# Attention and highway FFN on one core: the first duo by query blocks, the FFN in pairs of blocks, the last block in two column halves

## The chip, the cores and the metric

The kernel runs on one NeuronCore of a Trainium2 chip. The metric is the device time of one execution in microseconds (us). The time before the change is 175.32 us, the median of three runs (174.87 to 175.51). A profiled execution gives the trace that is read below; its span, from the first to the last instruction, is 173.5 us, and the granted TensorE clock is 0.987 on the mean.

Engines: PE is TensorE (PEld its weight loads), DVE VectorE, ACT ScalarE, POOL GpSimd, SP SyncE. Lxxx is a line of the kernel.

## The reference

Eight batches with eight heads of 576 positions and 64 dimensions go through sliding-window attention with an ALiBi bias. The heads are then joined to rows of 512, and each row goes through a highway layer with two 512 x 512 weights.

```python
def _attn_ref(q, k, v):                       # (8, 8, 576, 64) float32 each
    scale = 1.0 / np.sqrt(D); window = 128
    scores = scale * np.matmul(q, k.transpose(0, 1, 3, 2))
    rel = pos[:, None] - pos[None, :]
    slopes = 2.0 ** (-8.0 * (np.arange(H) + 1) / H)
    scores = np.where((rel >= 0) & (rel < window), scores - slopes * abs(rel), -1e9)
    attn = softmax(scores)
    return np.matmul(attn, v)

def _moe_ref(x, w_h, w_t, b_t):               # x: (4608, 512)
    H = np.maximum(x @ w_h, 0.0)
    T = 1.0 / (1.0 + np.exp(-(x @ w_t + b_t)))
    return T * H + (1.0 - T) * x              # = x + T * (H - x)
```

## The kernel before

Two batches make a duo (r = 0, 1), and there are four duos (m = 0 to 3). The 576 positions are four query blocks of 128 and a tail of 64; because of the window, block qb needs the keys of blocks qb - 1 and qb alone. A duo is worked through in stages, each of which names its pieces as (key block, query block, column):

```python
    STAGES = {
        "A": ((0, 0, 0), (0, 1, 128), (1, 1, 256), (1, 2, 384)),
        "B": ((2, 2, 0), (2, 3, 128), (3, 3, 256), (3, 4, 384), (4, 4, 448)),
        "a": ((0, 0, 0), (0, 1, 128)),
        "b": ((1, 1, 0), (1, 2, 128)),
        "c": ((2, 2, 0), (2, 3, 128)),
        "d": ((3, 3, 0), (3, 4, 128), (4, 4, 192)),
    }
    ORDER = ("abcd", "AB", "AB", "AB")
    GROUPS = {
        "A": ((0,), (1,), (2,), (3,)), "B": ((0,), (1,), (2,), (3,), (4,)),
        "a": ((0,), (1,)), "b": ((0,), (1,)), "c": ((0,), (1,)), "d": ((0,), (1,), (2,)),
    }
```

Loads of q, k and v go through GpSimd's DMA queue, which casts them from float32 to bfloat16. A q or k load takes four neighbouring positions to one partition, so a row of it is 256 elements; a V load takes 64. The first duo's first half comes in quarters by groups of heads. The weight w_h comes by SyncE in float32 ahead of everything and is cast by ScalarE.

```python
    def load_qk(m, w, x=None, hs=None):
        ...   # "h (p t) d -> p h (t d)", t=4: rows of 256 elements
            nc.gpsimd.dma_start(out=o, in_=i)
    def load_wf():
        nc.sync.dma_start(out=w_stage()..., in_=moe_w_h...)
    def cast_wf():
        nc.scalar.copy(out=wH[:]..., in_=w_stage())
```

For a stage and two heads (g): TensorE transposes q and k, makes the scores in two halves of 64 rows (one for each batch of the duo), ScalarE takes exp, VectorE multiplies with the mask, TensorE multiplies with V, which has a column of ones, and VectorE divides.

```python
                nc.tensor.transpose(out=pt[...], in_=L[ps, r, nh * hs + hl, ...], identity=ident[ps, ps])   # L271
                nc.tensor.matmul(out=sc[:, r, ...], lhsT=KT[...], rhs=rhs, ...)        # L329
        nc.scalar.activation(out=PT[...], in_=SC[...], func=ACTF.Exp, ...)             # L345
        nc.vector.tensor_tensor(out=o, in0=o, in1=mk..., op=ALU.mult)                  # L364
                            nc.tensor.matmul(out=av[...], lhsT=pt[...], rhs=va[...])   # L393
        nc.vector.reciprocal(...)                                                      # L409
        nc.vector.tensor_tensor(out=x..., in0=av..., in1=rd..., op=ALU.mult)           # L410
```

The FFN works on one block of 128 rows at a time (36 of them):

```python
                nc.tensor.transpose(out=pt[:, c * P : (c + 1) * P], ...)     # f_x, 4 of them, L433
        nc.scalar.copy(out=xt..., in_=TR...)                                 # f_xe, L442
            nc.tensor.matmul(out=AH, lhsT=XT..., rhs=wH[:, c, :], ...)       # f_h, 4, L449
        nc.vector.scalar_tensor_tensor(out=uu, in0=AH..., scalar=0.0, in1=x,
            op0=ALU.max, op1=ALU.subtract)                                   # f_u, L456
            nc.tensor.matmul(out=az, lhsT=XT..., rhs=wT[:, c, :], ...)       # f_z, 4, L465
        nc.tensor.matmul(out=az, lhsT=ones1[:], rhs=bT[:], ...)              # the bias, L467
        nc.scalar.activation(out=tt, in_=AZ..., func=ACTF.Tanh, scale=0.5)   # f_th, L473
        eng.tensor_scalar(out=tt, in0=tt, scalar1=0.5, scalar2=0.5, ...)     # f_t, L478
        nc.vector.tensor_tensor(out=uu, in0=uu, in1=tt, op=ALU.mult)         # f_g, L483
        eng.tensor_tensor(out=ot, in0=uu, in1=x, op=ALU.add)                 # f_out, L489
            nc.sync.dma_start(out=dst[t], ...)                               # f_st, 4, L505 (tail: 2, L497)
```

PSUM is one tile of eight banks, handed out bank by bank. The order of all steps and the bank of each are fixed lists of numbers in the kernel (ISSUE, BANKS), found beforehand; each engine keeps that order, and semaphores do the rest.

Of the kernel before, what the change touches and what calls it, by code (L numbers as in the profile page):

```python
# [14 lines left out]
def kernel(  # L15
# [30 lines left out]
        "a": ((0, 0, 0), (0, 1, 128)),  # L46
        "b": ((1, 1, 0), (1, 2, 128)),
        "c": ((2, 2, 0), (2, 3, 128)),
        "d": ((3, 3, 0), (3, 4, 128), (4, 4, 192)),
    }  # L50
    ORDER = ("abcd", "AB", "AB", "AB")
    DMA_X = ()

    HOME = {"A": ("A", 0), "B": ("B", 0), "a": ("A", 0), "b": ("A", 256), "c": ("B", 0), "d": ("B", 256)}

    GROUPS = {
        "A": ((0,), (1,), (2,), (3,)), "B": ((0,), (1,), (2,), (3,), (4,)),
        "a": ((0,), (1,)), "b": ((0,), (1,)), "c": ((0,), (1,)), "d": ((0,), (1,), (2,)),
    }

    ADD_MASK = ()
# [36 lines left out]
    def load_qk(m, w, x=None, hs=None):  # L98
        src, dst = ((q, QL), (k, KL))[w]
        ps = slice(0, P) if x is None else slice(64 * x, 64 * x + 64)  # L100
        for r in (slice(0, 2),) if hs is None else (0, 1):
            hh = slice(0, H) if hs is None else slice(4 * hs, 4 * hs + 4)
            if hs is None:
                o = dst[m % 2][ps].rearrange("p r h n -> p (r h) n")
                i = src[2 * m : 2 * m + 2, :, 4 * ps.start : 4 * ps.stop, :].rearrange(
                    "r h (p t) d -> p (r h) (t d)", t=4
                )
            else:
                o = dst[m % 2][ps, r, hh, :]
                i = src[2 * m + r, hh, 4 * ps.start : 4 * ps.stop, :].rearrange(  # L110
                    "h (p t) d -> p h (t d)", t=4
                )
            nc.gpsimd.dma_start(out=o, in_=i)  # L113
# [22 lines left out]
    MKA = ADD_MASK and cp.tile([P, H, 2 * P], BF16, name="mka")  # L136
    cvec = cp.tile([P, H], F32, name="cvec")
    ones1 = cp.tile([P, P], BF16, name="ones1")
    wH = cp.tile([P, NCK, DM], BF16, name="wH")
# [25 lines left out]


    BIG = float(2**20)

    def c_mka():
        nc.vector.tensor_scalar(out=MKA[:, :, 0:P], in0=bc(tri[:, 0, :], P), scalar1=BIG,  # L170
                                scalar2=-BIG, op0=ALU.mult, op1=ALU.add)
        for h in range(H):
            nc.vector.tensor_scalar(
# [127 lines left out]
    def width(kind):  # L301
        return 512 if kind in "AB" else 256
# [489 lines left out]
```

The softmax here doesn't subtract the row's maximum and nothing guards it: scores larger than these inputs give would overflow.

## Time and profile before

| what | before |
|---|---|
| time, median of 3 (lowest to highest) | 175.32 us (174.87 to 175.51) |
| profiled span | 173.5 us |
| TensorE busy | 150.3 us, 87% |
| VectorE busy | 140.0 us, 81% |
| ScalarE busy | 125.4 us, 72% |
| GpSimd busy | 118.1 us, 68% |
| DMA, GpSimd's queue | 62,832 packets, 14.68 MB |
| DMA, stores and w_h | 7,312 packets, 10.49 MB |

Busy time is the time in which an engine has an instruction in work. For TensorE it says little of how well it is filled, since matmuls overlap in its pipeline: the distance from one start to the next tells more. The groups of the profile give an instruction's line, engine, operation, tiles and count, then busy time and mean time of one, then the idle time ahead of it and what ended that. The chain is followed back from the last instruction, at each step to what released it.

### The profile page before, as it was taken

What the parts mean: (1) busy time and instruction counts of PE and PEld (TensorE: products, weight loads), DVE (VectorE), ACT (ScalarE), POOL (GpSimd) and SP (SyncE); (2) the same over time, 40 slices, a digit from 0 to 9 for tenths busy, and PEclk for the clock granted to TensorE, in tenths of its full rate; (3) what the DMA queues carried; (4) which work ended last, traced back from release to release, by engine and by line L of the source; (5) the groups of instructions that cost most, each with busy time, mean ns of one, the idle gap of its engine ahead of it and who ended that gap; (6) DMA issues with size and microseconds to landing.
All of it is one profiled execution on the core that took longest, in us unless ns stands there. A gap on an engine that the chain in (4) does not pass through costs nothing.

```text
span 173.5 us, 5255 instructions
## 1 busy us (share of the span) xinstructions
PE 150.3 (87%) x2132; PEld 92.8 (54%) x2132; DVE 140.0 (81%) x244; ACT 125.4 (72%) x178; POOL 118.1 (68%) x132
## 2 busy tenths in 40 slices
PE   0169789999799789999999979999999999999930
PEld 0158544666566347766556755566556556754410
DVE  5087686999898888999867999889887899976580
ACT  2625678797799969899779968799898897235510
POOL 7997373488883799984067985884485969676540
PEclk9999999999999999999999999999999999999995
DMA  4999999999999999999999996793124332454443
GB/s 161 211 191 191 154 197 185 184 176 102 190 205 202 197 108 158 216 217 210 252 118 154 153 179 97 88 135 99 45 64 121 76 90 68 107 127 113 125 121 91
DMA packets 70167, 25.50 MB, mean 147 GB/s; under 512 B 48128, under 2 KB 65024, under 8 KB 70144
## 3 DMA queue, kind: packets, MB, share of 16 engines
q0 software_dynamic: 62832, 14.68, 120.7%
q1 hardware_dynamic: 7312, 10.49, 22.6%
q8 instruction: 16, 0.26, 0.7%
q14 instruction: 7, 0.06, 0.1%
HBM read 30.41 MB, written 9.44 MB: 230 GB/s over the span
## 4 chain that ended last, share of the span: by engine, by line
PE 53%; DMA 29%; DVE 5%; POOL 4%; ACT 3%; issue 2%; SPq 0%; POOLq 0%; ACTq 0%; DVEq 0%
DMA va<-in_v_dram 17%; PE ps L465 14%; PE ps L449 14%; DMA ktl<-in_k_dram 8%; PE ps L393 7%; PE ps L329 7%; PE ps L271 4%; PE ps L433 4%; DMA kl<-in_k_dram 3%; PE ps L467 3%; ACT pt L345 2%; DVE pt L364 1%; POOL kl L113 1%; DVE uu L456 1%; DMA out_dram<-ot 1%
## 5 line engine op out<-in xcount | busy, mean ns | idle before, releaser
L345 ACT ACTIVATE pt<-ps,bias 128x1024 bf16<-128x1024 f32 (+1 forms) x80 | 72.2, 950 | 13.5 <-PE ps L329 13.2
L489 POOL TENSOR_TENSOR ot<-uu,x 128x512 f32<-128x512 bf16 x35 | 47.7, 1365 | 24.9 <-DVE uu L483 24.8
L364 DVE TENSOR_TENSOR pt<-pt,mk 128x2048 bf16<-128x2048 bf16 (+1 forms) x40 | 46.5, 1174 | 0.8 <-ACT pt L345 0.8
L465 PE MATMUL ps<-wT,xt 128*128 128x512 bf16 x144 | 37.0, 379 | 1.0 <-DVE uu L456 0.8
L449 PE MATMUL ps<-wH,xt 128*128 128x512 bf16 x144 | 37.0, 386 | 0.3 <-DVE qt L290 0.3
L473 ACT ACTIVATE tt<-ps 128x512 f16<-128x512 f32 x36 | 21.6, 602 | 13.0 <-PE ps L467 11.9
L456 DVE SCALAR_TENSOR_TENSOR uu<-ps,x 128x512 bf16<-128x512 f32 x36 | 24.5, 684 | 4.6 <-PE ps L449 4.3
L329 PE MATMUL ps<-qt,kt 64*128 64x256 bf16 (+2 forms) x384 | 24.8, 248 | 3.4 <-DVE qt L290 1.1
L478 POOL TENSOR_SCALAR tt<-tt 128x512 f16<-128x512 f16 x32 | 21.8, 687 | 7.7 <-ACT tt L473 7.5
L410 DVE TENSOR_TENSOR x<-ps,rd 128x256 bf16<-128x256 f32 (+3 forms) x40 | 25.5, 638 | 1.4
L125 POOL DMA_DIRECT2D va<-in_v_dram x20 | 22.3, 1115 | 5.6 <-DMA ql<-in_q_dram 4.2
L393 PE MATMUL ps<-va,pt 128*128 128x65 bf16 (+1 forms) x576 | 24.9, 197 | 0.8 <-DMA va<-in_v_dram 0.7
L393 PEld LDWEIGHTS <-pt 128*128 128x128 bf16 (+1 forms) x576 | 21.1, 101 | 8.2 <-issue 2.9
L442 ACT COPY xt<-ps 128x512 bf16<-128x512 bf16 x36 | 20.7, 589 | 5.3 <-PE ps L433 5.1
L483 DVE TENSOR_TENSOR uu<-uu,tt 128x512 bf16<-128x512 bf16 x36 | 19.1, 538 | 4.3 <-POOL tt L478 4.1
L449 PEld LDWEIGHTS <-xt 128*128 128x128 bf16 x144 | 13.0, 99 | 14.3 <-issue 2.1
L465 PEld LDWEIGHTS <-xt 128*128 128x128 bf16 x144 | 12.9, 98 | 13.6 <-issue 1.5
L329 PEld LDWEIGHTS <-kt 64*128 64x128 bf16 x384 | 13.2, 96 | 12.9 <-issue 8.9
L271 PE MATMUL ps<-ident,kl 128*64 128x128 bf16 (+1 forms) x320 | 12.3, 228 | 8.1 <-DMA kl<-in_k_dram 7.9
L296 ACT COPY kt<-ps 128x1024 bf16<-128x1024 bf16 x13 | 13.0, 1020 | 5.4 <-PE ps L271 5.4
L271 PEld LDWEIGHTS <-kl 128*64 128x64 bf16 (+1 forms) x320 | 9.9, 126 | 10.1 <-DMA kl<-in_k_dram 8.4
L290 DVE COPY qt<-ps 128x1024 bf16<-128x1024 bf16 x16 | 11.0, 686 | 3.8 <-PE ps L271 3.7
(44 smaller groups left out, 125.5 us busy)
## 6 DMA issues: line engine op xcount, KB each, us to landing
out_dram<-ot SPq DMA_DIRECT2D x128, 64.0 KB, 2.4
va<-in_v_dram POOLq DMA_DIRECT2D x16, 256.0 KB, 14.2
ql<-in_q_dram POOLq DMA_DIRECT2D x3, 1024.0 KB, 16.0
kl<-in_k_dram POOLq DMA_DIRECT2D x3, 1024.0 KB, 15.7
ql<-in_moe_w_h_dram SPq DMA_DIRECT2D x1, 1024.0 KB, 5.2
out_dram<-ot SPq DMA_DIRECT2D x8, 128.0 KB, 2.4
kl<-in_k_dram POOLq DMA_DIRECT2D x4, 128.0 KB, 5.5
ql<-in_q_dram POOLq DMA_DIRECT2D x4, 128.0 KB, 5.9
```

The source lines that it names most:

```text
L125: nc.gpsimd.dma_start(out=VA[m % 2][0:n, c, :, :, 0:D].rearrange("s r h d -> s (r h) d"), in_=v[2 * m : 2 * m + 2, :, c * P : c * P + n, : ...
L271: nc.tensor.transpose(out=pt[r * D : (r + 1) * D, c : c + n], in_=L[ps, r, nh * hs + hl, t * D : (t + 1) * D], identity=ident[ps, ps],)
L329: nc.tensor.matmul(out=sc[:, r, o + off : o + off + w_], lhsT=KT[i][rows, h, j * P : (j + 1) * P], rhs=rhs, start=not add, stop=not add or ...
L345: nc.scalar.activation(out=PT[m, home, h // 2][:, h % 2, :, c0 : c0 + W], in_=SC[m, kind, h][:, :, o : o + W], func=ACTF.Exp, bias=BIAS[:, ...
L364: nc.vector.tensor_tensor(out=o, in0=o, in1=mk.to_broadcast([P, 2, rep, W]), op=ALU.mult,)
L393: nc.tensor.matmul(out=av[rows, hl, n * (D + 1) : (n + 1) * (D + 1)], lhsT=pt[:, hl, r, off : off + (D if narrow else P)], rhs=va[:, j, r, ...
L410: nc.vector.tensor_tensor(out=x.rearrange("p b (h d) -> p h b d", h=2), in0=av[:, :, :, 0:D], in1=rd[:, :, 0:nb].to_broadcast([P, 2, nb, D ...
L449: nc.tensor.matmul(out=AH[m, kind, gi], lhsT=XT[m, kind, gi][:, i, c, :], rhs=wH[:, c, :], start=c == 0, stop=c == NCK - 1)
L456: nc.vector.scalar_tensor_tensor(out=uu[:, 0:n, :], in0=AH[m, kind, gi].rearrange("p (i n) -> p i n", i=1), scalar=0.0, in1=x, op0=ALU.max ...
L465: nc.tensor.matmul(out=az, lhsT=XT[m, kind, gi][:, i, c, :], rhs=wT[:, c, :], start=c == 0, stop=False)
L478: eng.tensor_scalar(out=tt, in0=tt, scalar1=0.5, scalar2=0.5, op0=ALU.mult, op1=ALU.add)
L489: eng.tensor_tensor(out=ot[:, 0:n, :], in0=UU.pop((m, kind, gi))[:, 0:n, :], in1=x, op=ALU.add)
```

## The change

The change has four parts and a new order.

1. The first duo goes by query blocks instead of by key blocks: stage e has query block 0, f block 1, g block 2, h block 3 and the tail. A stage is now complete in itself. The q and k of blocks 0 and 1 are loaded in their natural order, one position to a partition (rows of 64 elements), and are transposed with the full height of the array; the second half keeps the older form. This is meant to let the first blocks run through to the FFN without waiting for more of k.
2. w_h is loaded through GpSimd's queue with the cast, as w_t is; the copy by ScalarE goes.
3. The FFN works on two blocks with one instruction where it can (copy, u, tanh, t, gate), in two banks of PSUM. The two biases come from two matmuls of 64 rows each, which can run side by side, ahead of the z matmuls. This is meant to save fixed costs. The sum stays one block at a time; a store takes two blocks with four DMAs.
4. The very last block (the tail of the last duo) does z, tanh, t, gate, sum and store in two halves of 256 columns, one stored from SyncE and one from ScalarE. This is meant to shorten the end.

```diff
-        "a": ((0, 0, 0), (0, 1, 128)),
-        "b": ((1, 1, 0), (1, 2, 128)),
-        "c": ((2, 2, 0), (2, 3, 128)),
-        "d": ((3, 3, 0), (3, 4, 128), (4, 4, 192)),
+        "e": ((0, 0, 0),),
+        "f": ((1, 1, 0), (0, 1, 128)),
+        "g": ((2, 2, 0), (1, 2, 128)),
+        "h": ((2, 3, 0), (3, 3, 128), (3, 4, 256), (4, 4, 320)),
     }
-    ORDER = ("abcd", "AB", "AB", "AB")
+    ORDER = ("efgh", "AB", "AB", "AB")
...
-        "A": ((0,), (1,), (2,), (3,)), "B": ((0,), (1,), (2,), (3,), (4,)),
-        "a": ((0,), (1,)), "b": ((0,), (1,)), "c": ((0,), (1,)), "d": ((0,), (1,), (2,)),
+        "A": ((0, 1), (2, 3)), "B": ((0, 1), (2, 3), (4,)),
+        "e": ((0, 1),), "f": ((0, 1),), "g": ((0, 1),), "h": ((0, 1), (2,)),
...
+    def load_nat(w, b, hs):
+        src = (q, k)[w]
+        ...
+            nc.gpsimd.dma_start(
+                out=nat(w, b)[:, r, hh, :],
+                in_=src[r, hh, b * P : (b + 1) * P, :].rearrange("h s d -> s h d"),
+            )
...
-    def load_wf():
-        nc.sync.dma_start(
-            out=w_stage().rearrange("p (c n) -> p c n", c=NCK),
-            in_=moe_w_h.rearrange("(c p) n -> p c n", p=P),
-        )
-
-    def cast_wf():
-        nc.scalar.copy(out=wH[:].rearrange("p c n -> p (c n)"), in_=w_stage())
...
     def f_h(m, kind, gi, i):
-        AH[m, kind, gi] = ps_tile(1)
+        n = grp(m, kind, gi)[1]
+        if i == 0:
+            AH[m, kind, gi] = ps_tile(n).rearrange("p (i n) -> p i n", i=1) if n == 1 else ps_tile(n)
...
+    def f_zb(m, kind, gi):
+        AZ[m, kind, gi] = ps_tile(2)
+        for i in range(2):
+            rows = slice(i * D, (i + 1) * D)
+            nc.tensor.matmul(out=AZ[m, kind, gi][:, i, :], lhsT=hot2[rows, :], rhs=bT[rows, :],
+                             start=True, stop=False)
...
+    def e_z(m, kind, gi, hf):
+        if hf == 0:
+            AZ[m, kind, gi] = ps_tile(1)
+        az = AZ[m, kind, gi][:, half(hf)]
+        for c in range(NCK):
+            nc.tensor.matmul(out=az, lhsT=XT[m, kind, gi][:, 0, c, :], rhs=wT[:, c, half(hf)],
+                             start=c == 0, stop=False)
+        nc.tensor.matmul(out=az, lhsT=ones1[:], rhs=bT[:, half(hf)], start=False, stop=True)
...   # e_th, e_t, e_g, e_out in the same way, by halves
+    def e_st(m, kind, gi, hf, eng):
+        for r in range(2):
+            row = (2 * m + r) * S + 512
+            eng.dma_start(out=out[row : row + D, half(hf)],
+                          in_=OT[m, kind, gi][r * D : (r + 1) * D, 0, half(hf)])
...
-        eng.tensor_tensor(out=ot[:, 0:n, :], in0=UU.pop((m, kind, gi))[:, 0:n, :], in1=x, op=ALU.add)
+        eng.tensor_tensor(out=OT[m, kind, gi][:, i, :], in0=UU[m, kind, gi][:, i, :],
+                          in1=x[:, i, :], op=ALU.add)
...
     ISSUE = """    # the whole list is new, and so is BANKS
```

## The prediction

> **What bounds the kernel now.** I read the page's totals and its 40 slices, then the chain that ended last, then busy time by stretch, then the timeline of the end.
>
> ```profile
> PE 150.3 (87%) x2132; PEld 92.8 (54%) x2132; DVE 140.0 (81%) x244; ACT 125.4 (72%) x178; POOL 118.1 (68%) x132
> ...
> PE   0169789999799789999999979999999999999930
> ...
> DMA  4999999999999999999999996793124332454443
> ```
>
> TensorE is busiest, VectorE next. In the slices DMA is full from the second slice to about 104 us, and TensorE is full only from about a third of the span on. The chain, in order of time (start, length), says the same:
>
> ```profile
> 11.81 11.31 DMA va<-in_v_dram
> ...
> 26.31 17.49 DMA va<-in_v_dram
> ...
> 44.09 13.60 DMA ktl<-in_k_dram
> ...
> 130.51 0.33 PE ps L329 x8
> 130.84 0.97 PE ps L465 x4
> 131.81 0.22 PE ps L467
> ...
> 136.86 0.86 PE ps L465 x4
> ```
>
> Up to 57.7 us it is loads, afterwards nearly all TensorE. It also gives TensorE's real pitches: four 512-column matmuls take 0.86 (0.215 each), but 0.97 just after the 64-row scores of L329. So each change of array shape costs about 0.11 us. The mean of 379 ns in the groups is pipeline depth, not cost.
>
> Three stretches, cut at the first use of the second duo's V (61.6) and at the last probabilities-times-V (151.1); the columns are PE, PEld, DVE, ACT, POOL:
>
> ```profile
> 0.00:61.60 61.60, 48.34 (x795) 31.17 (x796) 46.42 (x99) 44.08 (x71) 43.02 (x60) 1.00 1.83 182
> 61.60:151.10 89.50, 86.86 (x1255) 54.45 (x1253) 80.77 (x123) 74.42 (x96) 64.03 (x62) 1.00 1.42 131
> 151.10:173.50 22.40, 15.11 (x91) 7.21 (x87) 12.78 (x25) 6.89 (x12) 11.06 (x11) 0.90 0.46 114
> ```
>
> The middle is TensorE's (97% busy), with VectorE at 90% close behind. Pricing each matmul by its pitch in a full stream (512 columns 0.2155; 128-column transposes 0.055; PV 0.029, narrow 0.020; one head's scores of a stage 0.22, since the two 64-row halves run side by side; q/k transposes 0.027, of 64 rows 0.033; tails 0.03), all of TensorE's work is 128.1 us: 38.4 in the first stretch, 75.0 in the middle, 14.7 at the end. In the middle about 80 shape changes at 0.11 make 9, which leaves some 5.5 for waits and small gaps.
>
> [...] Here, by the packet records, 128-byte packets (V) passed at about 1,000 per us in the best 4-us stretch, and 512-byte ones (q and k) at about 375, so 128 against 192 KB per us. [...]
>
> **The change, part by part.**
>
> FFN in pairs. (a) The bias: 36 matmuls become 16 pairs of half-height matmuls side by side, plus 4 single ones; 20 x 0.2155 instead of 36 x 0.2155 saves 3.45 us of TensorE. But they are 64-row matmuls. In the new order most sit beside scores of the same shape; still, changes of shape go from 130 to 140, 10 x 0.11 = 1.1 back. (b) Fixed costs, from these rows (count, then busy and mean ns):
>
> ```profile
> L456 DVE SCALAR_TENSOR_TENSOR uu<-ps,x 128x512 bf16<-128x512 f32 x36 | 24.5, 684 | 4.6 <-PE ps L449 4.3
> ...
> L478 POOL TENSOR_SCALAR tt<-tt 128x512 f16<-128x512 f16 x32 | 21.8, 687 | 7.7 <-ACT tt L473 7.5
> ...
> L483 DVE TENSOR_TENSOR uu<-uu,tt 128x512 bf16<-128x512 bf16 x36 | 19.1, 538 | 4.3 <-POOL tt L478 4.1
> ```
>
> [...] VectorE thus loses some 6 of 140. The ScalarE copies (two of 0.589 against 1.02, the mean of the 1,024-element k copies) give 16 x 0.16 = 2.5, tanh about 1, and the 1.9 us cast of w_h goes. [...] All but the bias lies beside TensorE and counts only where a wait ends on that engine.
>
> First duo by query blocks. 256 transposes of 64 rows become 128 of them and 64 of full height: 128 x 0.033 - 64 x 0.027 = 2.5 us less TensorE, all of it early, where TensorE waits anyway. In exchange k and q of blocks 0 and 1 arrive in 128-byte packets. They are 8,192 packets, 8.2 us at 1,000 per us, against 5.5 for the same bytes in 512-byte packets: 2.7 us more of a full DMA. The w_h load moves from SyncE, where it ran ahead of everything, to the GpSimd queue behind V: same traffic, later. Summing the new queue in its order from a first byte at about 4 us[...]: k and q block 0 land by about 15.7, q and k block 1 by about 19.8, w_h near 29.7, the second duo's q at 45.4, its first two V chunks near 57 and 59. The first exps start near 16 (14.15 now) and second-duo scores near 46 to 50 (43.1 now). ScalarE, to the second duo's sixth exp, has 22.3 us of first-duo exps (two forms of L345, 0.696 for 512 elements and 1.119 for 1,024, put 256 and 768 at 0.48 and 0.91), 6.7 of the second duo's, five k copies (5.1), a tail (0.6), q copies (2.1), and three pairs' copies and tanh (6.4): 43 us. It starts near 15 and idles about 2 us before block 1's k, so this also ends near 60. So the first second-duo PV comes at about 59.5: 2 us earlier than 61.6, but with only 33.0 us of TensorE work behind it instead of 38.4. What is saved early is spent on waiting; more FFN of the first duo is merely pushed back.
>
> Middle. The new order has 76.0 us of pitched work there, 85 changes at 0.11 = 9.4, and waits that I put at 4 instead of 5.5 since VectorE has 3.6 us less to do there (its rows there priced by the groups' means: 83.3 against 87.0). That is 89.4, as now, so the last PV falls at 148.9 instead of 151.1.
>
> The end, now:
>
> ```profile
> 158.99 10.17 SPq L505 DMA_DIRECT2D out_dram<-ot  x20
> ...
> 166.25 1.15 POOL L489 TENSOR_TENSOR ot<-uu,x 128x512 f32<-128x512 bf16 x1 [0.74 <-DVE uu L483]
> ...
> 168.05 0.69 DVE L489 TENSOR_TENSOR ot<-uu,x 128x512 f32<-128x512 bf16 x1
> 169.25 1.11 SPq L497 DMA_DIRECT2D out_dram<-ot  x2
> ```
>
> SyncE issues stores almost without pause, and the last block waits for it a little: sum ready at 168.74, issue at 169.25, end 3.1 us after the last issue (170.36). Pairs halve those issues and the column halves shorten the last block. But now a pair ends last. After the last PV TensorE has 13.2 us of pitched work and a few 0.1 us changes; the pair's last matmul comes 1.9 before the end of it (a block's H of 0.86 and the halves' 1.08 follow), near 11.5, and its tanh ends near 12.8. GpSimd does its L478 (1.1), VectorE the gate (0.8), GpSimd two sums of 1.15, and SyncE four issues of 0.42 (the median of its stores) behind the halves': last issue near 18.8, end 3.1 later, near 21.9, against 22.4 now. That is a gain of 0.5; the halves finish within the pair's shadow.
>
> Sum: span 148.9 + 21.9 = 170.8, plus the 1.8 by which the time exceeds the profiled span (175.32 - 173.5): 172.6. I round to 172.7.
>
> **Rivals.** First: the early DMA and ScalarE dictate. If ScalarE keeps only the 84 to 91% it shows now between 14 and 61.6 us, the first second-duo PV comes at 62 to 63 and everything shifts: 175 to 177. For it: the loads are full until 57.7 in the chain, and the new queue is longer. Against it: TensorE then has less left over and waits shrink. Second: the three other engines were what made TensorE wait, and with 4 to 5% off each the middle closes up and the end follows: 168 to 170. For it: VectorE at 90% beside TensorE, a 6 us stretch of the chain at 95 us on VectorE, and a total of TensorE that falls by 5.9 - 1.1 = 4.8 us. Against it: only some 5.5 us of real waits are there to win. Third: pairs hold two banks of PSUM through both halves, so with eight banks the scores wait longer for room: +2 to +4 us. The order and banks were chosen together, which speaks against much of it.
>
> **Range and chances.** The early part carries about +-2.5 us, the middle +-2, the end +-1: together about +-3.3, so 168.7 to 176.7 for eight in ten, somewhat wide because the early reckoning is made of landings. Two per cent is 171.8 and 178.8. Faster by over 2%: 0.38; within: 0.54; slower by over 2%: 0.08.
>
> **What would show it.** Bias row: 32 half-height matmuls, pitch about 0.22 a pair. L456's successor near 1.2 us, L483's near 0.75. First second-duo PV at 58 to 61 and last PV at 147 to 151 confirm the two dates. A chain that ends on GpSimd's last two sums and four SyncE stores confirms the end. The prediction fails if the first second-duo PV comes before 56 (loads cheaper than I reckon) or after 63, or if waits in the middle differ from 4 us by more than 3.

## The result: slower, and where it shows in the profile after

The changed kernel takes 180.66 us (180.2 to 180.9) where the kernel before took 175.09 beside it: a ratio of 1.031, 95% interval 1.028 to 1.034. The prediction was 172.7 us, at most 176.7 in eight of ten; it was wrong.

The page of the changed kernel, its totals and slices (the rows are PE, the granted clock, and the transfers with their GB/s):

```profile
PE 148.6 (83%) x2100; PEld 95.1 (53%) x2121; DVE 134.1 (75%) x216; ACT 121.8 (68%) x148; POOL 118.7 (66%) x122
...
PE   0368698999879889989999899999999999999500
...
PEclk9999999999978999999999999999999999999955
DMA  2999999999999999999299999952314402655543
GB/s 27 184 151 148 119 145 158 199 182 183 135 186 153 245 238 124 195 167 195 16 159 243 173 125 249 192 35 62 75 46 117 117 5 63 175 119 144 149 98 78
```

TensorE, VectorE and ScalarE have less to do than before, as predicted; GpSimd, which by an estimate of the author's was to save some 3 us, has 0.6 us more. 21 of 2,121 matmul records are missing. TensorE is thin until 27 us, the clock dips at 51 to 55 us, and the first slice moves 27 GB/s. In the kernel before, the first slice moved 161:

```profile
GB/s 161 211 191 191 154 197 185 184 176 102 190 205 202 197 108 158 216 217 210 252 118 154 153 179 97 88 135 99 45 64 121 76 90 68 107 127 113 125 121 91
```

The three stretches, cut at the first PV (probabilities times V) of the second duo and at the last PV:

```profile
0.00:62.50 62.50, 47.62 (x777) 33.19 (x783) 44.80 (x96) 41.43 (x63) 46.99 (x61) 0.97 1.76 158
62.50:154.10 91.60, 87.26 (x1245) 55.05 (x1256) 77.09 (x104) 74.39 (x78) 58.42 (x51) 1.00 1.26 130
154.10:179.00 24.90, 13.71 (x90) 6.86 (x88) 12.25 (x18) 6.03 (x8) 13.24 (x12) 0.84 0.51 127
```

So 62.5, 91.6 and 24.9 us: against the prediction (59.5, 89.4, 21.9) 3.0, 2.2 and 3.0 too long, together the 8 us of the miss; against the kernel before (61.6, 89.5, 22.4) 0.9, 2.1 and 2.5.

Cutting the middle once more, at the 217th of 576 PV matmuls, shows more. Pitched work is the sum of the prediction's prices; for the changed kernel it is taken from the run *x1_store_last*, which has all its records and the same program order.

| | before | changed | *x1*, same order |
|---|---|---|---|
| to the 145th PV (first of the second duo) | 61.6 | 62.5 | 63.6 |
| 145th to 217th | 15.7 | 17.7 | 16.7 |
| 217th to the last (576th) | 73.7 | 73.8 | 74.0 |
| after the last PV | 22.4 | 25.0 | 25.0 |
| pitched work in first part / middle / end | 38.5 / 75.0 / 14.7 | | 32.9 / 76.1 / 13.2 |
| FFN blocks whose H falls there | 8 / 21 / 7 | | 6 / 24 / 6 |

The pairs save work, but in the first part TensorE doesn't set the pace, and there two blocks fewer get done; three more than before stand in the middle. From the 217th PV to the last, the work is 62.7 us in the kernel before and 63.0 in *x1*, and the times are as near: 73.7, and 73.8 or 74.0. Between the 145th and the 217th there is 0.8 us more of it (13.06 against 12.22).

### The profile page after: what moved, and what is told of

Same layout as the page of the kernel before. It is cut to its first block, busy times and chain, and to the rows that moved or that the text cites. A ratio compares the mean times of both kernels' runs of the same rounds, so it can differ in the third digit from the quotient of the medians.

```text
span 179.0 us, 5012 instructions
## 1 busy us (share of the span) xinstructions
PE 148.6 (83%) x2100; PEld 95.1 (53%) x2121; DVE 134.1 (75%) x216; ACT 121.8 (68%) x148; POOL 118.7 (66%) x122
## 4 chain that ended last, share of the span: by engine, by line
PE 49%; DMA 17%; DVE 14%; POOL 9%; issue 4%; ACT 2%; DVEq 0%; POOLq 0%
PE ps L466 15%; PE ps L492 12%; DMA va<-in_v_dram 12%; PE ps L404 8%; PE ps L343 7%; DVE pt L375 6%; DMA kl<-in_k_dram 4%; POOL kl L115 3%; POOL ot L557 3%; PE ps L285 3%; DVE x L421 3%; PE ps L447 2%; PE ps L483 1%; DVE uu L473 1%; ACT pt L358 1%
## 5 line engine op out<-in xcount | busy, mean ns | idle before, releaser
L358 ACT ACTIVATE pt<-ps,bias 128x1024 bf16<-128x1024 f32 (+3 forms) x80 | 72.3, 947 | 19.9 <-PE ps L343 18.7
L557 POOL TENSOR_TENSOR ot<-uu,x 128x512 f32<-128x512 bf16 x35 | 45.1, 1304 | 22.7 <-DVE uu L551 20.1
L375 DVE TENSOR_TENSOR pt<-pt,mk 128x2048 bf16<-128x2048 bf16 (+3 forms) x40 | 43.7, 1110 | 5.9 <-ACT pt L358 5.9
L546 POOL TENSOR_SCALAR tt<-tt 128x1024 f16<-128x1024 f16 (+1 forms) x18 | 19.8, 1102 | 15.8 <-ACT tt L541 13.1
L473 DVE SCALAR_TENSOR_TENSOR uu<-ps,x 128x1024 bf16<-128x1024 f32 (+1 forms) x20 | 22.3, 1115 | 9.2 <-PE ps L466 7.8
L343 PE MATMUL ps<-qt,kt 64*128 64x128 bf16 (+2 forms) x432 | 25.7, 242 | 3.9 <-DVE qt L314 1.5
L141 POOL DMA_DIRECT2D va<-in_v_dram x20 | 22.2, 1111 | 9.8 <-DMA ql<-in_q_dram 7.5
L404 PE MATMUL ps<-va,pt 128*128 128x65 bf16 (+1 forms) x576 | 25.4, 200 | 2.1 <-DVE qt L297 0.9
L541 ACT ACTIVATE tt<-ps 128x1024 f16<-128x1024 f32 (+1 forms) x19 | 18.2, 958 | 9.8 <-PE ps L492 9.8
L343 PEld LDWEIGHTS <-kt 64*128 64x128 bf16 x432 | 15.8, 99 | 14.0 <-issue 10.6
L457 ACT COPY xt<-ps 128x1024 bf16<-128x1024 bf16 (+1 forms) x20 | 18.5, 932 | 3.9 <-PE ps L447 3.7
L466 PEld LDWEIGHTS <-xt 128*128 128x128 bf16 x144 | 13.2, 99 | 14.9 <-issue 1.4
L492 PEld LDWEIGHTS <-xt 128*128 128x128 bf16 x140 | 12.1, 98 | 15.2 <-issue 3.7
L551 DVE TENSOR_TENSOR uu<-uu,tt 128x1024 bf16<-128x1024 bf16 (+1 forms) x19 | 13.4, 714 | 2.4 <-POOL tt L546 2.4
L420 DVE RECIPROCAL rd<-ps 128x4 f32<-128x4 f32 (+3 forms) x40 | 8.0, 199 | 8.2 <-PE ps L404 7.7
L447 PE MATMUL ps<-ident,x 128*128 128x128 bf16 x144 | 11.6, 225 | 0.6 <-DVE x L421 0.5
## 6 DMA issues: line engine op xcount, KB each, us to landing
ktl<-in_k_dram POOLq DMA_DIRECT2D x8, 64.0 KB, 10.2
```

Of the source, the lines that this page charges most:

```text
L141: nc.gpsimd.dma_start(out=VA[m % 2][0:n, c, :, :, 0:D].rearrange("s r h d -> s (r h) d"), in_=v[2 * m : 2 * m + 2, :, c * P : c * P + n, : ...
L343: nc.tensor.matmul(out=sc[:, r, o + off : o + off + w_], lhsT=KT[i][rows, h, j * P : (j + 1) * P], rhs=rhs, start=True, stop=True,)
L358: nc.scalar.activation(out=PT[m, home, no, h // 2][:, h % 2, :, c0 : c0 + W], in_=SC[m, kind, h][:, :, o : o + W], func=ACTF.Exp, bias=BIA ...
L375: nc.vector.tensor_tensor(out=o, in0=o, in1=mk.to_broadcast([P, 2, rep, W]), op=ALU.mult,)
L404: nc.tensor.matmul(out=av[rows, hl, n * (D + 1) : (n + 1) * (D + 1)], lhsT=pt[:, hl, r, off : off + (D if narrow else P)], rhs=va[:, j, r, ...
L466: nc.tensor.matmul(out=AH[m, kind, gi][:, i, :], lhsT=XT[m, kind, gi][:, i, c, :], rhs=wH[:, c, :], start=c == 0, stop=c == NCK - 1)
```

## The experiments

The ratio is to the kernel before, from runs on one chip. The columns give the 145th PV, the two stretches after it and the end, from the profiled run (a dash: not read for that run). On the five chips the kernel before took 175.05 to 176.12 us (medians) beside these runs, so small steps are read with their intervals.

A date comes from one profile. Five runs share the changed kernel's program up to about 60 us (changed, *x1*, *x2*, *x8*, *z5*), and in them the 145th PV lies between 61.5 and 63.6 us and the 217th between 79.7 and 81.3. A shift of about 1 us in either therefore shows nothing by itself, the 0.9 us against the kernel before included. The last two columns are steadier: 73.7 to 74.0, and 24.9 or 25.0 in the runs (x1, x7, x9, x10, y2, z5) that leave the end as it is.

| run | ratio, 95% | 145th PV | to 217th | to last | end |
|---|---|---|---|---|---|
| changed | 1.031 (1.028-1.034) | 62.5 | 17.7 | 73.8 | 25.0 |
| *x1_store_last* | 1.033 (1.022-1.043) | 63.6 | 16.7 | 74.0 | 25.0 |
| *x2_whole_last* | 1.021 (1.011-1.031) | 63.4 | 17.9 | 73.8 | 23.2 |
| *x4_split* | 1.036 (1.026-1.046) | 62.4 | 17.4 | 74.5 | 24.6 |
| *x7_wh_sync* | 1.031 (1.022-1.039) | 63.3 | 17.0 | 73.9 | 24.9 |
| *x8_one_ring* | 1.025 (1.020-1.029) | 62.4 | 17.3 | 73.7 | 23.9 |
| *x9_warm* | 1.029 (1.025-1.033) | 62.5 | 18.3 | 74.1 | 25.0 |
| *x10_mask_early* | 1.028 (1.024-1.032) | 62.4 | 17.4 | 73.8 | 25.0 |
| *x5_bias_full* | 1.043 (1.040-1.047) | 62.8 | 17.2 | 76.2 | 25.3 |
| *y2_after_warm* | 1.022 (1.017-1.027) | 61.7 | 16.7 | 73.7 | 25.0 |
| *y3_after_all* | 1.019 (1.013-1.024) | 59.0 | 20.7 | 73.8 | 23.9 |
| *z1_wh* | 1.025 (1.020-1.029) | 62.0 | 16.7 | 74.5 | 23.8 |
| *z2_q3* | 1.029 (1.024-1.034) | 60.7 | 20.2 | 73.7 | 23.9 |
| *z3_both* | 1.020 (1.017-1.023) | 61.9 | 16.9 | 74.1 | 23.8 |
| *z5_sums* | 1.031 (1.025-1.038) | 61.5 | 18.1 | 73.7 | 25.0 |
| *z6_all_tail* | 1.023 (1.017-1.029) | 63.3 | 16.7 | 73.7 | 23.4 |
| before, *y1_before_warm* | 1.001 (0.998-1.004) | - | - | - | - |
| before, *y4_before_halves* | 1.004 (1.001-1.008) | - | - | - | - |
| before, *z4_before_wh* | 1.015 (1.012-1.018) | 64.0 | 15.8 | 73.7 | 22.0 |

### The end: rings, halves, and one semaphore

The changed kernel's store queue at the end (start, length, engine; the q marks issues), and SyncE's waits there:

```profile
170.78 1.11 SPq L534 DMA_DIRECT2D out_dram<-ot  x2
171.99 3.94 SPq L574 DMA_DIRECT2D out_dram<-ot  x4
```

```profile
SPq L574 <- DMA out_dram<-ot: 2.1, 1, 2.1
```

Four issues take 3.94 us, 2.1 of it a wait for a landing: the third of the last pair's stores uses the completion semaphore that ScalarE's first half store uses (number 111; the 74 stores of the trace use eight, 111 to 118, 9 or 10 times each), and waits for that store, issued at 172.66, to land: it lands at 175.13, and the issue starts at 175.14.

*x1_store_last*: half 1's store moved to the end of the list.

```diff
+    late = [k_ for k_ in order if k_[0] == "st" and len(k_) == 3 and k_[2] == 1]
+    order = [k_ for k_ in order if k_ not in late] + late
```

> The changed kernel, with the second column half's store moved from ahead of the last pair's stores to the very end of the list; the same stores on the same two rings. Theory of the lane: in the changed kernel SyncE stands from 172.57 to 175.14 us because the third store of the last pair takes its turn on a completion semaphore whose previous user is ScalarE's half store; behind the last store in the list nobody takes that turn, so SyncE's stores go out in one piece, and the end comes 1.5 to 2.5 us earlier: 178.2 to 179.2 us against 180.7. Rival, contention ([...]GpSimd's sums of the last pair set the end): the stores are the same, and the time stays within 0.5 us of 180.7.

Ratio 1.033; SyncE waits the same 2.1 us. The store already stood last in the list, so the edit moved nothing: this run is the changed kernel once more. But it shows that the semaphores are not handed out in that list's order.

*x8_one_ring*: both halves stored by SyncE.

```diff
-    e_st(*kb, hf, nc.scalar if hf else nc.sync)
+    e_st(*kb, hf, nc.sync)
```

> The changed kernel with both column halves of the last block stored by SyncE (the second half's store behind the last pair's four), nothing else moved. The run before this one had shown that the list already puts ScalarE's store last, and that it all the same holds the completion semaphore which the third store of the last pair waits for. Theory of the lane: with one ring that semaphore was last used long before, SyncE doesn't wait in the middle of the pair's stores, and the end comes 1.5 to 2.5 us earlier, 178.2 to 179.2 us (180.7 before the edit), although the second half's two stores (some 0.6 us each to issue) now stand in the same queue. Rival: the second ring is worth what it was made for, and the wait is hidden: 0 to 1 us slower, 180.7 to 181.7.

SyncE's queue in this run:

```profile
171.30 1.95 SPq L574 DMA_DIRECT2D out_dram<-ot  x4
173.35 1.11 SPq L534 DMA_DIRECT2D out_dram<-ot  x2
```

The four issues go out in 1.95 us and the end falls from 25.0 to 23.9: the second ring cost 1.1 us, less than the 2 expected because the second half's stores now stand behind the pair's.

*x2_whole_last*: the last block whole, one store.

```diff
-    return slice(256 * hf, 256 * hf + 256)
+    return slice(0, 512)          # and the steps of hf == 1 left out
```

> The changed kernel with its last block whole again (gate, tanh, sum on 512 columns, one store on SyncE's ring), everything else as it is. Theory of the lane: the store of ScalarE's ring is gone, so the wait is gone too; the last chain's operations are each 0.2 to 0.4 us longer, but the end comes from the last pair's stores: 1 to 2.5 us faster than the changed kernel (178.2 to 179.7). Rival, the halves are a real gain that something else hides: as slow as the changed kernel or up to 1.5 us slower (180.7 to 182.2).

The end is 23.2, some 0.7 less than with halves on one ring (the ratios, 1.021 and 1.025, overlap). So the halves themselves gain nothing here.

*y4_before_halves*: part 4 of the change alone, in the kernel before (z, tanh and so on by halves, half 1's store on ScalarE's ring).

```diff
+    put(("g", kb), lambda: [e_g(*kb, 0), e_out(*kb, 0), e_st(*kb, 0, nc.sync), e_t(*kb, 1)])
+    put(("o", kb), lambda: [e_g(*kb, 1), e_out(*kb, 1)])
+    put(("st", kb), lambda: e_st(*kb, 1, nc.scalar))
```

> The kernel before with the third part of the change alone: the last block's gate, tanh, sum and store in two column halves, the second half's store on ScalarE's ring; all else as before. Prediction's step: the halves let the first half's store go out while the second is worked on, 0.3 to 1 us faster than the kernel before. Theory of the ring: ScalarE's two stores take their turns on the eight completion semaphores in the middle of SyncE's row, and SyncE's last stores wait for them: 0.5 to 2 us slower. If the end is set by the pair before it in the queue, within 0.3 us.

0.4% slower (0.1 to 0.8), about 0.75 us, and without a semaphore wait: half 0's store goes out at 169.77 (1.11 us) ahead of the block before it, whose sum was over at 168.80, and that one's four stores start at 170.98. In the changed kernel two of VectorE's instructions also take longer at this point, beside GpSimd's sums:

```profile
168.41 0.23 DVE L518 TENSOR_SCALAR tt<-tt 128x256 f16<-128x256 f16 x1 [0.77 <-ACT tt L513]
...
169.32 2.44 POOL L557 TENSOR_TENSOR ot<-uu,x 128x512 f32<-128x512 bf16 x2 [1.11 <-DVE uu L551]
169.48 1.28 DVE L528 TENSOR_TENSOR ot<-uu,x 128x256 f32<-128x256 bf16 x1
170.68 1.17 DVE L518 TENSOR_SCALAR tt<-tt 128x256 f16<-128x256 f16 x1
...
172.21 0.42 DVE L528 TENSOR_TENSOR ot<-uu,x 128x256 f32<-128x256 bf16 x1
```

The same half sum takes 1.28 us beside GpSimd's sums and 0.42 after them; L518, 1.17 and 0.23. In *z6_all_tail* (below), where VectorE makes these sums itself, both half sums take 0.42 us and both of these affine steps 0.22 to 0.23.

### The grain and the bias

*x4_split*: each pair's copy, u, tanh, affine step and gate as two instructions.

```diff
-        nc.vector.scalar_tensor_tensor(out=uu[:, 0:n, :], in0=AH[m, kind, gi], ...)
+        for i in range(n):
+            nc.vector.scalar_tensor_tensor(out=uu[:, i, :], in0=AH[m, kind, gi][:, i, :], ...)
```

> The changed kernel with the copy, u, tanh, t and gate of each pair of blocks as two instructions of one block (same order, same PSUM banks, same matmuls). Theory of the grain: what waits for a pair's first block can begin 0.4 to 0.6 us earlier, and the mask and normalisation that stand behind a long VectorE instruction too; the 7.5 us of TensorE waits in the middle shrink by 1 to 2 us, 178.7 to 179.7 us against 180.7. Rival, fixed cost: 17 pairs x 2 instructions on VectorE, each about 0.1 to 0.15 us of fixed cost dearer, and the same on ScalarE and GpSimd, come back as 1 to 3 us: 181.7 to 183.7 us. If VectorE and ScalarE are off the bound, no more than 0.5 us either way.

```profile
PE 150.7 (84%) x2121; PEld 95.3 (53%) x2121; DVE 141.3 (79%) x249; ACT 123.4 (69%) x180; POOL 121.4 (68%) x137
```

VectorE is busy 7.2 us longer than in the changed kernel for 33 instructions more (0.22 each), 5.1 of it in the middle, and the time is not clearly another: 1.036 against 1.031, with intervals of about 1%. No gain from the finer grain is seen, and this 7.2 us comes back in the time at most in part: the stretch from the 217th PV to the last, where TensorE is the bound, is 0.7 us longer (74.5). A loss of 1 or 2 us in all is not excluded.

*x5_bias_full*: each block's bias as one full-height matmul.

```diff
-            nc.tensor.matmul(out=AZ[...][:, i, :], lhsT=hot2[rows, :], rhs=bT[rows, :], ...)   # f_zb
-        if one:
+        if True:
             nc.tensor.matmul(out=az, lhsT=ones1[:], rhs=bT[:], start=False, stop=True)
```

> The changed kernel with the bias of each block again as one matmul of full height behind its four z matmuls (two of 0.216 us for a pair of blocks, in place of two half-height ones that run side by side in 0.22 us with a change of array shape of about 0.1 us before and after). Theory of the prediction: the pair form saves 0.1 to 0.2 us for each of 16 pairs, 12 to 14 of them in stretches where TensorE is the bound: 1.5 to 2.5 us slower without it, 182.2 to 183.2. Rival: the shape changes eat what the side-by-side matmuls save, or other waits absorb it: within 0.7 us of 180.7.

1.2% slower than the changed kernel (1.043 to 1.031), 2.1 us, and 2.4 of it lies between the 217th and the last PV (76.2 for 73.8). This is shown: there TensorE is the bound and the paired bias earns what the prediction gave it (3.45 - 1.1 = 2.35).

### The first part: the cold clock, the mask, and what each hid

The clock row shows 9 from the start, but it has no record before 30.9 us in the changed kernel (28.9 before). The pitch, the distance from one start to the next, shows more. PV matmuls, 0.029 us apart in the middle, are 0.054 apart from 21.4 to 25.4 us before and from 21.9 to 29.8 in the changed kernel. From the chain of *x7_wh_sync*, two times four h matmuls of 512 columns:

```profile
30.75 1.41 PE ps L468 x4
...
33.06 0.98 PE ps L468 x4
```

The first four run partly at half clock. In the kernel before its first h matmuls start at 27.45, 27.88, 28.30 and 28.73 us, 0.43 apart, and the next at 29.05, 29.27, 29.48, 29.70, 0.216 apart. So TensorE works at half clock there and leaves it 1 to 1.5 us after the first h products, which start at 27.45 us before and at 29.87 in the changed kernel (the clock's first record, of 1.0, starts at 28.94 and 30.86). Earlier pitches agree: pairs of 256-column score halves are mostly 0.213 us apart from 13.0 us in the kernel before, and 0.119 at the median after 31 us; pairs of 128-row transposes of k and q are 0.107 us apart from 9.3 us in the changed kernel, and 0.056 later (medians). The transposes and scores from 9 to 28 us did not end the half clock, although those of the kernel before ran from 13.0 to 18.1 us without a pause of over 0.15 us. Then, 15 us later, the chain of the changed kernel:

```profile
47.03 1.69 PE ps L466 x7
...
49.02 0.69 DVE uu L551
...
49.78 1.10 POOL ot L557
50.88 20.84 DMA va<-in_v_dram
```

TensorE stands from 48.9 to 50.35 us because the bank it needs is freed by a q copy behind these on VectorE (first fence, changed; second, before):

```profile
44.57 0.47 DVE L221 COPY mk<-tri 128x1024 bf16<-128x1024 bf16 x1
44.96 0.67 DVE L215 TENSOR_TENSOR mk<-tri,cvec 128x512 bf16<-128x512 bf16 x1
45.55 1.65 DVE L221 COPY mk<-tri 128x512 bf16<-128x512 bf16 x1
47.24 1.85 DVE L375 TENSOR_TENSOR pt<-pt,mk 128x1536 bf16<-128x1536 bf16 x1
```

```profile
12.71 0.55 DVE L215 COPY mk<-tri 128x1024 bf16<-128x1024 bf16 x1
13.19 0.67 DVE L209 TENSOR_TENSOR mk<-tri,cvec 128x512 bf16<-128x512 bf16 x1
13.78 0.28 DVE L215 COPY mk<-tri 128x512 bf16<-128x512 bf16 x1
```

The new order builds half of the mask 32 us later, just ahead of work that TensorE waits for, and one copy takes 1.65 us there instead of 0.28. GpSimd issues v loads beside it (44.71 to 47.08 us); but beside the 0.28 it issued loads too (tails, 13.00 to 14.39), so the cause was not shown. Just after, the clock falls to half from 51.3 to 54.7 us.

*x10_mask_early*: the mask's second half at 30 us.

```diff
+    order.remove(("mask1",))
+    order.insert(order.index(("nrm", (0, "f", 1))) + 1, ("mask1",))
```

> The changed kernel with the three VectorE instructions that build the second half of the mask moved from 45.6 us (where they hold VectorE for 2.7 us, in front of a mask, a gate and the q copy that frees the PSUM bank TensorE waits for) to about 31 us, where VectorE waits 1.9 us for TensorE; in the kernel before they ran at 12.7 to 14.1 us. Theory of the place: TensorE's 1.7 us wait at 49.7 goes, the first second-duo PV comes 1.5 to 2.5 us earlier (60 to 61 us), and the time falls by 1.5 to 2.5 us: 178.2 to 179.2. Rival: the start of the second duo is set by transfers or by ScalarE, and the gain is lost at the next wait: less than 0.5 us, 180.2 to 180.9.

*x9_warm*: filler where TensorE stands.

```diff
+        if (m, kind, h) == (0, "h", 7):
+            for _ in range(8):
+                nc.tensor.matmul(out=sc[:, 0, :], lhsT=ident[:], rhs=wH[:, 0, :], start=True, stop=True)
```

> The changed kernel with eight extra 128x512 matmuls (1.7 us at full clock, their result is overwritten) on TensorE in front of the last scores of the first duo, where TensorE stands 1.7 us waiting for VectorE at 49.7 to 51.4 us. Theory of the clock: the granted clock falls to 0.5 for 3.4 us at 51 to 55 us[...]; filled up, the stretch of 0.5 goes and the time falls by 0.5 to 1.5 us (179.2 to 180.2). Rival: the clock isn't granted by what TensorE did just there, or the stretch is not on the bound: no gain, or up to 0.5 us slower (180.7 to 181.2).

Neither brings the 145th PV forward (62.4 and 62.5). In the filler's profile there is no half-clock stretch at 51 us, but that doesn't show that the filler kept the clock: *x8* has the same program there without filler and the same wait of 1.5 us (49.3 to 50.8), no such stretch either, and its 145th PV at 62.4. So the dip itself costs nothing that the date shows. With the mask moved, the wait for VectorE is gone, yet TensorE stands 1.7 us at 48.9 without a cause in the trace, and the clock falls all the same. Both rivals held.

*y1_before_warm* and *y2_after_warm*: full-height filler in TensorE's early gaps, in the kernel before and in the changed one.

```diff
+    FILL = {('tr', 0, 1, (1, 1)): 16, ('tr', 0, 1, ('n0', 0)): 4, ('tr', 0, 0, ('n1', None)): 2,
+            ('tr', 0, 1, ('n1', None)): 4, ('s', 0, 'f', 4): 3, ('s', 0, 'f', 6): 1, ('pv', (0, 'f', 0)): 1}
+    # n matmuls of 512 columns into the next bank ahead of each of these steps
```

> The kernel before with 24 extra 128x512 matmuls of a tile of ones, whose result is overwritten, in places of the first 27 us where TensorE stands idle: 14 ahead of its first transposes, then 4, 3, 2 and 1. Theory of the cold clock: the traces show each 512-column matmul of the h products at 0.43 us until 28.9 us in the kernel before and until 30.9 to 32.7 us in the changed one, and at 0.216 us from then on; [...] Full-height filler releases it at 6 to 9 us, TensorE's first 20 us of work take half the time, and the end comes 1 to 3 us earlier: 172.0 to 174.5 us (before 175.1 to 176.1 on this chip). Rival: the first part is set by transfers, exps and the masks, and the released clock only makes TensorE wait: within 0.6 us of the kernel before. Second rival: between the fillers the clock falls back to half, and nothing changes but the order of a few tenths.

> The changed kernel with 31 such fillers in the places of its first 29 us where TensorE stands idle (16 ahead of the first transposes, then 4, 2, 4, 3, 1, 1). Theory of the cold clock: its half-clock stretch lasts 2 to 4 us longer than the kernel before's, because the first h products wait for w_h until 29.9 us; released early, the time falls by 1.5 to 3.5 us, 177.2 to 179.2 us against 180.7. Rival, the first part is set by the loads and ScalarE: within 0.6 us of 180.7.

In the kernel before: nothing (1.001). In its profile the clock was full from 7.4 us, but half again from 14.2 to 21.0 and from 24.4 to 27.8, as the second rival had it (mean clock 0.957 there, 0.94 to 0.97 in its other executions); so what a lasting full clock is worth there stays open. In the changed kernel it was full from 5.1 to 11.9 and from 22.2 us on, and the time fell by about 0.9% (1.022 for 1.031).

*y3_after_all*: y2, x10, x8 and four fillers of x9's at once.

> The changed kernel with four edits at once: the fillers of the run before this one, four more ahead of the last first-duo scores (49.7 us), the second half of the mask built at 31 us and not at 45.6, and both column halves stored by SyncE. Theory: the repairs that brought little one by one (0.3 and 0.4 us for the filler and the mask) did so because each left the other's wait in place, and together with the clock they are worth 3 to 6 us: 174.7 to 177.7. Rival: only the single ring counts (1.3 us), the rest is lost at the next wait: 178.8 to 179.8.

Now the clock was full from 7.9 to 69.4 us, and the 145th PV came at 59.0 us, the prediction's 59.5; in z2, which has the same repairs, it came at 60.7. Both lie outside the 61.5 to 63.6 of the unrepaired program. Of these 3.5 us only 0.6 was left at the 217th: 20.7 us passed instead of 17.7. The end kept x8's 1.1. In all it is 1.2% faster than the changed kernel, 2.3 us by the ratios: less than the theory's 3 to 6, and no more than the fillers of y2 (0.9%) and the one ring of x8 (0.6%) gained separately. Its median, 179.0, lies within the rival's range. The chain, and the waits from 66 to 70 us, name the new wait:

```profile
46.79 22.66 DMA ql<-in_q_dram
...
69.49 1.92 PE ps L287 x16
```

```profile
POOL va L141 <- DMA ql<-in_q_dram: 7.7, 1, 7.7
...
PE ps L287 <- DMA ql<-in_q_dram: 2.5, 1, 2.5
```

The third duo's q, issued at 46.8 us, needs 22.7 us to land, at 69.5; in the kernel before it was issued at 36.3 and had landed at 53.1. The 16 transposes that waited for it then take 1.92 us (0.57 in the kernel before), while the clock was at half again, from 69.4 to 72.8 us. How much of the 3.0 us lost is the wait and how much the clock is not separated.

### The transfers' queue

*z4_before_wh*: in the kernel before, w_h through GpSimd's queue, as the change has it.

```diff
-        nc.sync.dma_start(out=w_stage()..., in_=moe_w_h...)     # load_wf, and cast_wf's copy
+        nc.gpsimd.dma_start(out=wH[:], in_=moe_w_h.rearrange("(c p) n -> p c n", p=P))
+    order.insert(order.index(("w", 1)), ("wf",))
```

> The kernel before with one part of the change alone: w_h comes through GpSimd's queue as bf16 (issued at about 14 us, behind the first tails and ahead of w_t), and SyncE's load with ScalarE's cast is gone. Theory of the queue: every load behind it lands 2 to 4 us later while the queue is full, and the kernel before becomes 1 to 3 us slower (176.5 to 178.5). Rival, the prediction's: the cast of 1.9 us is gone from ScalarE ahead of the first exps and the same bytes come either way: 0 to 1.5 us faster (173.5 to 175.2).

1.5% slower, 2.6 us, nearly all of it (2.3) before the 145th PV. The first slices of its transfers, with those of the kernel before shown above:

```profile
GB/s 47 130 166 185 154 203 199 170 194 130 156 200 213 201 144 124 219 229 187 260 151 155 117 148 155 62 124 117 64 65 94 70 93 73 115 103 123 129 121 105
```

SyncE's load had moved its packets from 1.9 to 5.7 us, while GpSimd was still issuing its first loads: 161 GB/s then, 47 here, 27 in the changed kernel. By the packet records it came almost for nothing: by 16 us GpSimd's queue had moved 1.96 MB beside it and 2.04 MB without it. The bytes put off stand later in a full queue: in *z4*'s row of DMA shares every slice from the second to the 25th, up to 109.6 us, shows 9.

*x7_wh_sync*: the reverse, in the changed kernel.

```diff
+    def load_wf():  # nc.sync.dma_start of moe_w_h into QL[1] as float32, first in the list
+    def cast_wf():  # nc.scalar.copy into wH, behind the bias table
```

> The changed kernel with w_h loaded as in the kernel before: SyncE brings float32 into the free q buffer at the start, ScalarE casts it (1.9 us); the other early loads move up by one transfer of 1 MB on GpSimd's queue. Theory of the queue: the first second-duo PV (62.5 us) is late because the natural 128-byte-row loads and w_h share GpSimd's queue with the halves of q and k; with w_h off that queue the second-duo PV comes 1 to 2.5 us earlier and the time is 178.2 to 179.7. Rival, ScalarE: the cast's 1.9 us stand in front of the first exps and the first duo's time is set by the order of VectorE and ScalarE, not by the loads: 0 to 1.5 us slower, 180.7 to 182.2.

No change (1.031): the queue gains, but the first exps come at 17.0 us instead of 15.1, and the first load of k, now beside w_h, takes 8.1 us from issue to landing instead of 6.0.

*z1_wh*: y3 with w_h by SyncE (the edit of x7). *z2_q3*: y3 with the third duo's q ahead of v's fourth block. *z3_both*: both.

```diff
+    order.remove(("qk", 2, 0, None))
+    order.insert(order.index(("v", 1, 3)), ("qk", 2, 0, None))
```

> The changed kernel with the four edits of the run before (fillers, mask early, one ring), and w_h again brought by SyncE as float32 at the start and cast by ScalarE. In the first 4 us the transfers of the changed kernel move 27 to 30 GB/s, of the kernel before 161. Theory of the queue: with w_h out of GpSimd's queue every load behind it lands 3 to 4 us earlier; the third duo's q at 65 to 66 us instead of 69.5, TensorE's wait at 67 us goes, and the time falls by 2 to 4 us against those four edits alone: 175 to 177 us. Rival: the first exps come 2 us later for it, and the order needs the rest of the queue just as late: 178.5 to 179.5 us.

> The changed kernel with those four edits, and the third duo's q load issued ahead of the second duo's fourth block of v, not behind it and a sum: 2 to 3 us earlier. Theory of the place: q lands at 66 to 67 us, TensorE's 2.7 us wait goes, and the time falls by 1.5 to 3 us, 176 to 177.5 us. Rival, the amount: the queue is full until about 70 us, so the v blocks that now stand behind q land where q did, and the second PV stage of the second duo waits for them instead: 178.5 to 179.5 us.

> Both of the two runs before at once: w_h by SyncE and the third duo's q ahead of v's fourth block, on top of the four edits. Theory of the queue: 174.5 to 176.5 us, as fast as the kernel before or a little faster. Rival (the amount of bytes, not the place or w_h): 178 to 179.5 us.

z2 is no faster than y3. TensorE's wait for q is gone, and it waits for v instead (waits from 70 to 75 us), and here too a half-clock stretch follows, from 73.6 to 77.1 us:

```profile
POOL va L141 <- DMA va<-in_v_dram: 3.3, 2, 2.3
...
PE ps L406 <- DMA va<-in_v_dram: 1.8, 1, 1.8
```

So the place of q is not the cause; moving it moves the wait. z1 and z3 have no such wait (16.7 and 16.9 us to the 217th), but their first exps come at 16.6 and 17.3 us instead of 15.2, and their 145th PV at 62 again. z3, at 1.020, is level with y3. That fits a full queue, in which what one load gains another loses, but it does not prove the amount of bytes to be the cause: *y2*, with w_h in GpSimd's queue and its 145th PV at 61.7, has no wait for a load there either.

*z5_sums*: two sums of the first duo ahead of the two v loads they stood behind in GpSimd's list. *z6_all_tail*: z3 and z5, with the last pair's affine step and sums on VectorE.

```diff
+    for key in [("o", (0, "g", 0), i) for i in range(2)]:
+        order.remove(key)
+        order.insert(order.index(("v", 2, 1)), key)
+    # z6 also: f_t and f_out of the last pair with nc.vector for nc.gpsimd
```

> The changed kernel with one edit: the two sums of the first duo's third pair (gate done at 60.6 us, sums at 73.4 us) stand ahead of the third duo's first two v loads in GpSimd's list, not behind them. Theory of the list: the norm that waited for them at 74.7 to 75.7 us goes on at once, the PV groups behind it come 1 to 1.5 us earlier (79 us against 80.2), and the end too: 179.2 to 179.7 us against 180.7. Rival: the wait is only the last of several (transfers land at 70 us all the same): within 0.5 us of 180.7.

> All repairs at once on the changed kernel: fillers, mask early, one ring, w_h by SyncE, the third duo's q ahead of v's fourth block (178.7 us so far), and now the two sums ahead of the v loads, and the affine step and the two sums of the last pair of blocks on VectorE (0.43 and 2 x about 0.65 us there, 1.04 and 2.4 us on GpSimd). Theory: 1 us from the sums in the middle, 1 to 1.5 us from the tail: 176 to 177 us, still no faster than the kernel before. Rival: the tail's stores are what counts (eight of 0.45 us on one queue), and VectorE has its own work there: 177.8 to 178.7.

z5: no clear change; the norm's wait for the sums was only the last of several. z6: no better than z3; the end shrinks by 0.4, not by 1 to 1.5. No version of the changed kernel reached the kernel before.

## Why the prediction was wrong, step by step

Three terms of the prediction's sum failed, each by 2 to 3 us: the date of the first second-duo PV, the waits in the middle, and the queue of stores at the end.

**Prices: right, GpSimd's saving apart.** A bias pair 0.22 us (its two matmuls start 0.003 to 0.018 us apart), u of a pair 1.222 (put at 1.2), its gate 0.734 (0.75), the first H at 29.87 (w_h "near 29.7"), first exps at 15.06 ("near 16"). x5 measured the bias at 2.1 us. What a pair saves on VectorE and GpSimd was the author's estimate, from no row of the kernel before. Measured, it is 0.15 us for u (2 x 0.684 - 1.222), 0.34 for the gate (2 x 0.538 - 0.734) and 0.32 for GpSimd's affine step (2 x 0.687 - 1.054); VectorE has 5.9 us less in all ("some 6"), while GpSimd as a whole has no less.

**"So the first second-duo PV comes at about 59.5": 62.5.** The loads were reckoned well: block 1's q and k landed by 19.0 us (19.8), the second duo's q at 44.7 (45.4), its first two v blocks at 57.8 and 59.9 (57 and 59). ScalarE, put down for 43 us of work and 2 of idling, was busy 38.2 us and idle 9.3 from 15.0 to 62.5, 7.0 of that waiting for TensorE's scores. What the step left out was TensorE's clock, priced full from the start while it was half until 30.9 us, and VectorE's order, in which half of the mask had moved to 44.6 us. With clock, mask and gap repaired together the date was 59.0 (60.7 in z2); singly they gave 0 to 0.8 us, which is within the spread, so the shares stay open. The first rival (62 to 63, 175 to 177 us in all) had the date; its reason, that ScalarE sets the pace, was not shown.

**"What is saved early is spent on waiting; more FFN of the first duo is merely pushed back": right, and underrated.** The middle got its 76.0 us of pitched work as reckoned (76.1). That is 1.1 more than before, so the pairs could not shorten it.

**"Waits that I put at 4 instead of 5.5 since VectorE has 3.6 us less to do there": this step failed.** By the prediction's own split, the middle's 91.54 us less 76.06 of pitched work and 9.35 of shape changes (85 of 0.11) leave 6.1 us; the four runs with the same program up to the last PV (changed, x1, x2, x8) give 5.3 to 6.3, and the kernel before 5.4. So the waits did not shrink. x4 speaks against the reason: with 5.1 us more of VectorE's work in the middle, its length was 91.9 us, hardly more. What the middle has beyond the kernel before lies almost wholly before the 217th PV, 0.8 us of it more work; after it both kernels run alike.

**"Same traffic, later": the same bytes, but 2.6 us.** z4 measured it in the kernel before. The reckoning followed the queue from its first byte at 4 us and missed that SyncE's load had used the time from 1.9 to 5.7 us. In the changed kernel the reverse (x7) gained nothing, so the 2.6 us are not simply a part of the 5.6.

**The end, "near 21.9": 25.0.** The last issue was to be over 18.8 us after the last PV and was over at 21.9; the end follows 3.1 us later, as reckoned. Of the 3.1 us between the two dates, 2.1 are the wait for a completion semaphore shared with the other ring. The prediction had placed the pair's four stores behind the first half's, but not behind a landing of the second half's. One ring gained 1.1 of it (x8), the whole block a further 0.7 (x2). VectorE's half sum took 1.28 us beside GpSimd's sums, which put off the first half's store; in z6, without these sums on GpSimd, the end was 0.4 shorter.

**Open:** why x10's TensorE stands 1.7 us without a recorded cause; how much of the 1 to 2 us between the 145th and 217th PV belongs to each transfer; what the natural-row loads of k and q, with 6,736 more packets in the queue than before, cost by themselves, and what the new order does: no run took either out. The third rival, that pairs hold two banks of PSUM and the scores wait for room, was not tested by itself; waits of 5.3 to 6.3 us in the middle against 5.4 before leave it about 1 us there. So the losses are placed and partly measured, but they don't add up piece by piece to the 5.6 us.

## What to carry to other kernels

Work saved on an engine counts only in the stretch where that engine is the bound: cut the span at the dates that matter, and ask for each stretch what it holds before and after, since what no longer fits early is done later at full price. When a new order is searched, look in each engine's list for setup work that has slipped onto the critical stretch, and for loads that leave the first microseconds empty while a queue is full later. A second store ring is not free: its stores may share completion semaphores with the first one's, and then one ring waits for the other's landing (2.1 us here).

## What the runs showed of the hardware that was not expected

- TensorE worked at half clock until 28.9 us before and 30.9 in the changed kernel, by all pitches that can be compared (from 13.0 and 9.3 us on), in spite of dense transposes and scores, until 1 to 1.5 us after the first 128x512 matmuls (PV 0.054 us apart, then 0.029). With filler of that form the clock was full from 7.4 us (y1), 5.1 (y2) and 7.9 (y3), and it fell back for 3.4 to 10.2 us at a time.
- A store waited 2.1 us for a store of the other ring through a shared completion semaphore (172.66 to 175.13 us in the changed kernel).
- Two of VectorE's instructions took three and five times as long beside GpSimd's sums as after or before them (1.28 us for 0.42, 1.17 for 0.23). A copy took 1.65 us for 0.28; its cause was not shown.
